# A gated-delta recurrence and a mixture of experts on one core: chunks of 64 tokens in 12 turns in place of 32 tokens in 24

## The chip, the core and the metric

The kernel runs on one core of a Trainium2 chip. The metric is the time of the whole kernel in microseconds on the device. Engines in the profile: PE is TensorE's matmuls and PEld its weight loads, DVE is VectorE, ACT is ScalarE, POOL is GpSimd, SP issues most of the transfers.

## What is computed

A DeltaNet layer (4 batches, 8 heads, 768 tokens, head size 48) is followed by a mixture of 8 experts with one expert per token. All is float32.

```python
for t in range(S):
    y[:, :, t] = einsum('bhd,bhde->bhe', q[:, :, t], state)
    v_old = einsum('bhde,bhd->bhe', state, k_n[:, :, t])
    state = state + beta_t * einsum('bhd,bhe->bhde', k_n[:, :, t], v[:, :, t] - v_old)
x = y.transpose(0, 2, 1, 3).reshape(3072, 384)
expert = argmax(x @ w_gate);  gate = softmax(x @ w_gate)[expert]
out = gate * (relu(x @ w1[expert]) @ w2[expert])
```

`k_n` is k divided by its length. The 32 pairs of batch and head are independent; the tokens of a pair depend on each other through `state` (48 x 48).

## The kernel before, in words

**Chunks and turns.** The 768 tokens of each pair are cut into chunks of C = 32 tokens, and all 32 pairs take one chunk in one of NT = 24 turns. In a chunk, the sequence of single steps becomes matrix work: the keys' products with each other (scores, L255) give a lower triangular matrix; its inverse (`invert`, L309 to L375) is applied to what the values lack against the state. Partitions are four groups of 32 rows, the columns are 8 pairs (FQ) of 48.

**One turn**, in the order in which the parts need each other: the state times keys and, for the outputs of the chunk before, the state times queries (`with_state`, L456, 128 matmul records into banks BR and BY); VectorE subtracts this from the scaled values, R (L489); the inverse times R and, interleaved with it, the masked products that complete the outputs of the chunk before (L502 and `masked`, L463); ScalarE copies the result as Z (L513); keys times Z are added to the state (`kz`, L518) in two banks that hold the state throughout; ScalarE copies it out as S (L526). Beside it `output` copies the finished outputs, stores them to `xs` in DRAM, transposes them (L549), multiplies them by the gate weights (L562), and `route` finds each token's expert and place (L594 to L645).

**Inverse.** `invert` works on four chunks at a time (a block, six in all): VectorE transposes the scores (L309), finds the lengths of the keys, and eliminates 31 columns with two operations each (L355 and L360). For the first block it eliminates two halves of 16, which TensorE then joins (`couple`, L397 and L404). Scores run up to 12 turns ahead (AHEAD, with RING = 14 buffers).

**Experts.** When all tokens are routed, the lists are loaded, tokens are gathered by list, transposed (L740), and each of 8 experts runs two dense products (L754, L800) for up to 416 tokens; a loop behind it serves more. The weights of the first two experts are loaded during the turns, the third's after.

**Order.** Each operation is entered in a `Plan` with an engine, an estimated duration and a priority; `order` plays a schedule through and writes the instructions in the order of the planned starts. An engine executes in that order. `mode` adds 0.12 us in the plan when TensorE changes its tiling.

## Time and profile before

| | us |
|---|---|
| median of 3 runs | 690.65 (689.38 to 692.21) |
| the profiled execution | 689.81 |
| its span, first to last instruction | 688.1 |
| first Z / last Z | 51.93 / 346.32 |
| first product of an expert | 383.88 |

The profile describes one execution, which took 689.81 us, of which the span covers 688.1. A float32 product leaves two matmul records and a transpose one. In rows of the windows by stage the columns are the stretch and its length, then for each engine busy time and number of instructions, the mean granted clock of TensorE (1.00 is full), the share of time in which the DMA engines were busy, and the GB/s that they moved. In rows of the timeline they are the start, the duration, engine, line, operation, operands and count, and in brackets the idle time ahead and what ended it; "issue" stands where the trace shows nothing that was waited for. Queue rows have packets, megabytes and share of time.

### The profile page before, as it was taken

The page shows a single profiled execution, that of the slowest core. Times are in us where ns is not written, and L with a number is a line of the kernel's source. Part 1 is how long each engine was busy: PE and PEld are TensorE (multiplying, and loading weights), DVE is VectorE, ACT ScalarE, POOL GpSimd, SP SyncE. Part 2 cuts the span into 40 slices and gives each one's busy share as a digit, 9 for nine tenths or more (in the row PEclk, how much of TensorE's full clock was granted, in tenths as well). Part 3 has the DMA queues.
Part 4 walks back from the last instruction along what each step waited for, and adds up shares of the span by engine and source line. Part 5 has one row for each costly group of instructions (what it writes and reads, how often), then busy time and mean ns, then how long its engine had stood idle before and what let it go on. Part 6 is the DMA issues. An engine that isn't in the chain of part 4 may idle for free. (4 is left out here: it accounts for less than half of the span.)

```text
span 688.1 us, 24689 instructions
## 1 busy us (share of the span) xinstructions
PE 539.0 (78%) x11376; PEld 371.4 (54%) x11377; DVE 234.1 (34%) x728; ACT 116.7 (17%) x267; POOL 133.2 (19%) x157
## 2 busy tenths in 40 slices
PE   3575665678587767678770899999999999999992
PEld 2464555567476656567660555555555555555551
DVE  3886755886877662001010101021011101021110
ACT  1222232213222122122210101101110101010100
POOL 1123111122232120210202504030302222101111
PEclk9999567557765655555555899999999999999997
DMA  8406544453322134331010324243433322000000
GB/s 311 157 5 212 162 126 140 144 169 82 106 50 55 51 61 116 96 95 40 15 26 13 92 104 150 92 144 103 143 114 112 102 101 97 23 15 23 13 12 23
DMA packets 36075, 63.58 MB, mean 92 GB/s; under 512 B 6102, under 2 KB 27014, under 8 KB 35968
## 3 DMA queue, kind: packets, MB, share of 16 engines
q1 hardware_dynamic: 30928, 51.62, 24.6%
q0 software_dynamic: 4352, 9.47, 4.2%
q8 instruction: 90, 1.47, 0.9%
q10 hardware_dynamic: 688, 0.88, 0.4%
q14 instruction: 17, 0.14, 0.1%
HBM read 52.68 MB, written 10.05 MB: 91 GB/s over the span
## 5 line engine op out<-in xcount | busy, mean ns | idle before, releaser
L754 PE MATMUL bk<-kqA,w 128*128 128x416 f32 x288 | 102.7, 515 | 0.0
L800 PE MATMUL bk<-w,kqA 128*128 128x384 f32 x288 | 96.1, 490 | 0.0
L754 PEld LDWEIGHTS bk<-kqA,w 128*128 128x128 f32 x288 | 54.5, 192 | 45.0 <-issue 43.3
L355 DVE SCALAR_TENSOR_TENSOR bk<-blkA,b 128x60 f32<-128x60 f32 (+22 forms) x185 | 76.8, 415 | 4.6
L800 PEld LDWEIGHTS bk<-w,kqA 128*128 128x128 f32 x288 | 53.7, 190 | 42.5 <-issue 7.5
L255 PE MATMUL bk<-kqA 64*32 64x64 f32 (+1 forms) x1792 | 47.5, 272 | 29.8 <-issue 19.6
L502 PE MATMUL bk<-R,blkA 32*32 32x48 f32 x1472 | 45.3, 252 | 26.4 <-issue 22.7
L759 DVE TENSOR_SCALAR kqA<-bk 128x416 f32<-128x416 f32 x32 | 18.9, 591 | 133.9 <-PE bk L754 110.4
L711 POOL DMA_INDIRECT out<-y,rows x24 | 23.9, 994 | 206.5 <-ACT y L773 162.6
L456 PE MATMUL bk<-S,kqA 64*32 64x48 f32 x2944 | 48.4, 270 | 13.4 <-issue 11.3
L255 PEld LDWEIGHTS bk<-kqA 64*32 64x32 f32 x1792 | 38.7, 150 | 35.6 <-issue 22.8
L463 PE MATMUL bk<-Z,P 32*32 32x48 f32 x1536 | 46.5, 253 | 14.4 <-issue 14.4
L360 DVE TENSOR_TENSOR blkA<-blkA,bk 128x60 f32<-128x60 f32 (+22 forms) x185 | 54.1, 312 | 2.7
L456 PEld LDWEIGHTS bk<-S,kqA 64*32 64x32 f32 x2944 | 41.0, 138 | 22.1 <-issue 14.8
L518 PE MATMUL bk<-Z,kt 32*48 32x48 f32 x1472 | 37.9, 277 | 18.6 <-issue 11.1
L502 PEld LDWEIGHTS bk<-R,blkA 32*32 32x32 f32 x1472 | 36.1, 128 | 28.4 <-issue 23.5
L489 DVE TENSOR_TENSOR R<-vn,bk 128x384 f32<-128x384 f32 x23 | 12.7, 553 | 107.1 <-PE bk L456 100.3
L463 PEld LDWEIGHTS bk<-Z,P 32*32 32x32 f32 x1536 | 37.1, 129 | 19.6 <-issue 19.6
L518 PEld LDWEIGHTS bk<-Z,kt 32*48 32x48 f32 x1472 | 33.0, 185 | 23.2 <-issue 12.6
L436 POOL TENSOR_TENSOR vn<-v,nt 128x384 f32<-128x384 f32 x24 | 21.0, 877 | 121.0 <-DVE R L489 103.0
L645 POOL DMA_INDIRECT lists<-ent,ri x24 | 24.2, 1007 | 98.0 <-DVE ri L633 61.5
L770 DVE TENSOR_SCALAR y<-bk,rows 128x384 f32<-128x384 f32 x8 | 4.9, 618 | 92.1 <-PE bk L800 92.1
(103 smaller groups left out, 576.1 us busy)
## 6 DMA issues: line engine op xcount, KB each, us to landing
kqA<-in_kq SPq DMA_DIRECT2D x20, 512.0 KB, 7.2
w<-in_w SPq DMA_DIRECT2D x18, 512.0 KB, 5.8
w<-in_w SPq DMA_DIRECT2D x12, 768.0 KB, 5.5
kt<-in_ktok SPq DMA_DIRECT2D x24, 192.0 KB, 2.6
v<-in_vtok SPq DMA_DIRECT2D x24, 192.0 KB, 3.4
xs<-x SPq DMA_DIRECT2D x48, 96.0 KB, 2.6
blkA<-in_w SPq DMA_DIRECT2D x6, 512.0 KB, 4.8
blkA<-in_w SPq DMA_DIRECT2D x4, 768.0 KB
```

Of the source, the lines that this page charges most:

```text
L255: nc.tensor.matmul(dst[32 * q : 32 * q + 32, f, :].rearrange("p (k c) -> p k c", c=32), lhsT=v[rows, 0, x * FQ + f, :], rhs=v[rows, ks[0] ...
L355: dve(m * w, lambda col=col, hi=hi, lo=lo, m=m, w=w, pv=pv: nc.vector.scalar_tensor_tensor(out=pv, in0=gl[:, col + 1 : hi, col : col + 1]. ...
L360: dve(m * w, lambda col=col, hi=hi, lo=lo, w=w, pv=pv: nc.vector.tensor_tensor(out=u[:, col + 1 : hi, lo : lo + w], in0=u[:, col + 1 : hi, ...
L436: lambda: nc.gpsimd.tensor_tensor(out=v2s[t % 3][:], in0=vs[t % 3][:], in1=nt[:, u * FQ : u * FQ + FQ].unsqueeze(2).to_broadcast([128, FQ, ...
L456: nc.tensor.matmul(dst[quad(col), f, :], lhsT=KQ(t)[64 * e : 64 * e + 64, k, x * FQ + f, :], rhs=Sbs[t % 2][64 * e : 64 * e + 64, x, f, :] ...
L463: nc.tensor.matmul(sh(BY)[quad(q ^ 2), f, :], lhsT=Pbs[t % RING][quad(q), f, :], rhs=Zbs[t % 2][quad(q), f, :], start=start, stop=True, sk ...
L502: nc.tensor.matmul(pz[quad(q), f, :], lhsT=tt[quad(q), u * FQ + f, :], rhs=Rv[quad(q), f, :], start=True, stop=True,)
L518: nc.tensor.matmul(sh(BS[x])[64 * e : 64 * e + 48, f, :], lhsT=kt[quad(q), f, :], rhs=Z[quad(q), f, :], start=(t == 0 and f == 0), stop=Tr ...
L645: P.op("POOL", 1.0, lambda i=i: nc.gpsimd.indirect_dma_start(out=lists, out_offset=bass.IndirectOffsetOnAxis(ap=ri[:, i : i + 1], axis=0), ...
L711: nc.gpsimd.indirect_dma_start(out=out, out_offset=bass.IndirectOffsetOnAxis(ap=idx, axis=0), in_=src, in_offset=None, bounds_check=N - 1, ...
L754: nc.tensor.matmul(bk[b][:, 0:CAP], lhsT=a1[:, s, f * 128 : f * 128 + 128], rhs=xT[:, s, :], start=(s == 0), stop=(s == NK - 1))
L800: nc.tensor.matmul(bk[b][:, 0:DM], lhsT=hT[:, f, t * 128 : t * 128 + 128], rhs=a2[:, f, :], start=(f == 0), stop=(f == NF - 1))
```

## The change

Chunks have 64 tokens (C = 64), in NT = 12 turns. The partitions of a product are two groups of 64 rows, one for each e, and the outputs go to two groups of 64 and to a pair of adjacent banks, one for each e. PSUM is four pairs: state, residual (BR), inverse (BZ) and outputs (BY). Scores share BY with the outputs; transposes, logits and ranks share BZ with the inverse.

A turn solves its 64 tokens in two steps of 32. The values enter BR by two products with the identity (`values`); the state times keys is added to them in place; VectorE and ScalarE copy one bank each as R; the first half's inverse gives Z; `across` adds the coupling of the halves to BR; R is copied again; the second half's inverse gives the rest of Z; then kz and S as before. The outputs' products with the state and with the masked scores are now separate groups of 64 records. The keys' signs and the order of the halves are turned for odd e, so that the rows of each product lie in their own lanes.

`invert` takes two chunks of 64 as a block, still six blocks, with diagonal 32 x 32 blocks that four DMAs collect in `GD`. The scaling by beta comes ahead of the elimination, the products of the elimination lie in SBUF instead of PSUM, and the first block is eliminated whole; `couple` is gone. RING is 6 and AHEAD is 4. The weights of the first three experts take buffers of the recurrence and are loaded when these are free. Keys and queries are loaded without zero rows, in four transfers a turn. In the plan, `mode` gives way to `passes`: after every 128 matmuls the next block can't end before 3.4 us.

The core of the diff, with the new side of the turn:

```diff
-C = 32
+C = 64
...
-NB = NT // 4
+NB = NT // 2
...
-RING = 14
-AHEAD = 12
+RING = 6
+AHEAD = 4
+PAGE, FILL = 128, 3.4
...
-            eng, cost, _, _, _, mode, lat = self.ops[i]
-            if mode is not None and mode != last.get(e):
-                cost += 0.12
-                last[e] = mode
+            eng, cost, _, _, _, passes, lat = self.ops[i]
             start[i] = t
+            end = t
+            if passes:
+                each = cost / passes
+                while passes:
+                    k = min(passes, PAGE - page)
+                    end += k * each
+                    passes -= k
+                    page += k
+                    if page == PAGE:
+                        page = 0
+                        end = max(end, filled)
+                        filled = end + FILL
+            else:
+                end += cost
+            free[e] = end
...
+    pairs = [pp.tile([128, 2, 512], FP32, name=f"pair{i}") for i in range(4)]
+    bk = [pairs[i // 2][:, i % 2, :] for i in range(8)]
+    BS, BR, BZ, BY = 0, 2, 4, 6
...
+            for g in range(2):
+                P.op("PE", 0.9, lambda g=g: run(BY, (0, 1), range(4 * g, 4 * g + 4)), r=kKQ(t), w=kb(BY),
+                     prio=t - AHEAD + 0.5 + 0.01 * g, passes=32)
+                src = pairs[3][:].rearrange("p e (f c) -> p e f c", f=4)
+                P.op("ACT", 0.6, copy(
+                    "ACT",
+                    xy[:, :, 16 * u : 16 * u + 16].rearrange("p c (e f) -> p e f c", e=2)[:, :, 4 * g : 4 * g + 4, :],
+                    src[:, :, :, 0:C]),
+                    r=kb(BY), w=[("XY", n % 3, u, g)], prio=t - AHEAD + 0.5)
+                P.op("ACT", 0.6, copy("ACT", Pm(t)[:, :, 4 * g : 4 * g + 4, :], src[:, :, :, C:]),
+                     r=kb(BY), w=[("P", t % RING)], prio=t - AHEAD + 0.5)
+        later = const("later").rearrange("p (e c) -> p e c", e=2).unsqueeze(2).to_broadcast([128, 2, FQ, C])
         P.op(
...
+        for q in range(4):
+            s = q % 2
+            e, k = (nc.scalar, "ACT") if n == 0 and s else (nc.sync, "SP")
+            P.op(k, 0.6, dma(e, flat(GD[quad(q)]), flat(xy[quad(q), 32 * s : 32 * s + 32, :])),
+                 r=kXY(n), w=[("GD", q)], prio=pr - 3, lat=2.3)
...
+            r, w = slice(16 * h, 16 * h + 16), 16 * h + 16
+            dve(16 * w, lambda r=r, w=w: nc.vector.tensor_tensor(
+                out=gl[:, r, 0:w], in0=gl[:, r, 0:w], in1=b[:, r].unsqueeze(2).to_broadcast([128, 16, w]),
+                op=OP.mult), [K("b")], [kgl], pr)
+        dve(32, lambda: nc.vector.tensor_copy(out=flat(u)[:, 0:1024:33], in_=b[:]), [K("b")], [ku], pr)
+        for j in range(31):
+            m, w = 31 - j, j + 1
+            pv = prods[n % 2][:, 0 : m * w].rearrange("p (a b) -> p a b", b=w)
+            dve(m * w, lambda j=j, m=m, w=w, pv=pv: nc.vector.tensor_tensor(
+                out=pv, in0=gl[:, j + 1 : 32, j : j + 1].to_broadcast([128, m, w]),
+                in1=u[:, j : j + 1, 0:w].to_broadcast([128, m, w]), op=OP.mult),
+                [kgl, ku], [("prod", n % 2)], pr)
+            dve(m * w, lambda j=j, w=w, pv=pv: nc.vector.tensor_tensor(
+                out=u[:, j + 1 : 32, 0:w], in0=u[:, j + 1 : 32, 0:w], in1=pv, op=OP.subtract),
+                [("prod", n % 2)], [ku], pr)
...
+    def with_state(t, bank, k, first):
+        for f, e, x in products():
+            nc.tensor.matmul(
+                sh(bank + e)[half(x), f, :], lhsT=KQ(t)[feat(e), k, x * FQ + f, :],
+                rhs=Sbs[t % 2][feat(e), x, f, :], start=first and f == 0, stop=True,
+                skip_group_check=True,
+            )
...
+        def values():
             for e in range(2):
+                nc.tensor.matmul(
+                    bk[BR + e][:, 0:DM], lhsT=const("ident"),
+                    rhs=v2s[t % 2][:, e * FQ : e * FQ + FQ, :].rearrange("p f d -> p (f d)"),
+                    start=True, stop=True, skip_group_check=True,
+                )
+        P.op("PE", 1.3, values, r=[("v2", t % 2), "cf"], w=kb(BR), prio=t - 0.3, passes=4)
         if t:
+            P.op("PE", 1.0, lambda: with_state(t, BR, 0, False), r=kKQ(t, (0,)) + kS, w=kb(BR), prio=t, passes=64)
+        def residual(i):
+            for e in range(2):
+                P.op("ACT" if e else "DVE", 0.45, copy(
+                    "ACT" if e else "DVE", Rbs[i][:, e].rearrange("p f d -> p (f d)"), bk[BR + e][:, 0:DM]),
+                    r=[("bk", BR + e)], w=[("R", i, e)], prio=-90)
+        def inverse(i):
+            def run():
+                for f, e, x in products():
+                    q = 2 * x + (e ^ i)
                     nc.tensor.matmul(
+                        sh(BZ + e)[quad(q), f, :], lhsT=tt[quad(q), 16 * u + 8 * e + f, :],
+                        rhs=Rbs[i][quad(q), e, f, :], start=True, stop=True, skip_group_check=True,
                     )
+            P.op("PE", 0.8, run, r=kT + [("R", i, e) for e in range(2)], w=kb(BZ), prio=t, passes=64)
+            P.op("ACT", 0.75, copy("ACT", both(Z), two(BZ), -1.0), r=kb(BZ), w=[("Z", t % 2)], prio=-90)
+        def across():
+            for f, e, x in products():
+                q = 2 * x + e
+                nc.tensor.matmul(
+                    sh(BR + e)[quad(q ^ 1), f, :],
+                    lhsT=xy[quad(q), 32 * (1 - e) : 32 * (1 - e) + 32, 16 * u + 8 * e + f],
+                    rhs=Z[quad(q), e, f, :], start=False, stop=True, skip_group_check=True,
+                )
+        residual(0)
+        inverse(0)
+        P.op("PE", 0.8, across, r=kXY(n, (u,)) + [("Z", t % 2)], w=kb(BR), prio=t, passes=64)
+        residual(1)
+        inverse(1)
         if t < NT - 1:
             def kz():
+                for f, e, x in products():
                     nc.tensor.matmul(
+                        sh(BS + x)[feat(e), f, :], lhsT=kt[half(x), e * FQ + f, :],
+                        rhs=Z[half(x), e, f, :], start=(t == 0 and f == 0), stop=True,
                         skip_group_check=True,
                     )
+            P.op("PE", 1.2, kz, r=[("kt", t % 2), ("Z", t % 2)], w=kb(BS), prio=t, passes=64)
+            for x in range(2):
+                P.op("ACT", 0.45, copy(
+                    "ACT", Sbs[(t + 1) % 2][:, x].rearrange("p f d -> p (f d)"), bk[BS + x][:, 0:DM]),
+                    r=[("bk", BS + x)], w=[("S", (t + 1) % 2, x)], prio=-90)
+    def output(t):
         if t:
+            P.op("PE", 1.0, lambda: with_state(t, BY, 1, True), r=kKQ(t, (1,)) + [("S", t % 2, x) for x in range(2)],
+                 w=kb(BY), prio=t + 0.6, passes=64)
+            P.op("ACT", 0.2, copy("ACT", between[:].rearrange("p (e f) -> p e f", e=2),
+                                  two(BY).rearrange("p e (f d) -> p e f d", d=D)[:, :, :, 0]),
+                 r=kb(BY), w=["between"], prio=-80)
+        def masked():
+            for f, e, x in products():
+                nc.tensor.matmul(
+                    sh(BY + e)[half(x), f, :], lhsT=Pm(t)[half(x), e, f, :], rhs=Zbs[t % 2][half(x), e, f, :],
+                    start=(t == 0 and f == 0), stop=True, skip_group_check=True,
                 )
+        P.op("PE", 1.0, masked, r=[("P", t % RING), ("Z", t % 2)], w=kb(BY), prio=t + 0.6, passes=64)
+        for h in range(2):
+            i = 2 * t + h
+            P.op("ACT", 0.45, copy(
+                "ACT", xbs[i % 3][:].rearrange("p (e c) -> p e c", e=2),
+                pairs[BY // 2][:, :, 192 * h : 192 * h + 192], -1.0),
+                r=kb(BY), w=[("x", i % 3)], prio=t + 0.6)
+            P.op("SP", 0.6, dma(nc.sync, xs[i * 128 : i * 128 + 128, :], xbs[i % 3][:]),
+                 r=[("x", i % 3)], w=[("xs", i)], prio=t - 3)
+    def logits(t):
+        for h in range(2):
+            i = 2 * t + h
+            x, xT, b = xbs[i % 3], xTs[i % 2], BZ + h
+            def tx(x=x, b=b):
+                for s in range(NK):
+                    nc.tensor.transpose(
+                        bk[b][:, s * 128 : s * 128 + 128], x[:, s * 128 : s * 128 + 128], const("ident"))
+            P.op("PE", 0.7, tx, r=[("x", i % 3), "cf"], w=[("bk", b)], prio=t + 1.2, passes=6)
+            P.op("ACT", 0.45, copy("ACT", xT[:].rearrange("p a b -> p (a b)"), bk[b][:, 0:DM]),
+                 r=[("bk", b)], w=[("xT", i % 2)], prio=t + 0.7)
+            def lg(xT=xT, b=b):
+                for s in range(NK):
+                    nc.tensor.matmul(bk[b][:, 0:E], lhsT=xT[:, s, :], rhs=wg[:, s, :], start=(s == 0), stop=(s == NK - 1))
+            P.op("PE", 0.6, lg, r=[("xT", i % 2), "wg"], w=[("bk", b)], prio=t + 1.2, passes=6)
+            m, j = group_of[i]
+            P.op("ACT", 0.2, copy("ACT", lgs[m % 2][:, j, :], bk[b][:, 0:E]),
+                 r=[("bk", b)], w=[("lg", m % 2, j)], prio=t + 0.7)
...
+    weights(0, 8)
+    weights(1, 20)
     weights(2, 21)
```

## The prediction

> **What bounds the kernel now.** I read the time slices of the page first, then the windows by stage, then TensorE's timeline, then the instruction queue. The first view splits the 688.1 us span.
>
> ```profile
> core 0: us, PE busy (x) PEld busy (x) DVE busy (x) ACT busy (x) POOL busy (x), PEclk, DMA share, GB/s
> 0.00:52.00 52.00, 27.64 (x1370) 24.56 (x1372) 35.30 (x123) 10.48 (x25) 10.31 (x23) 1.00 0.44 156
> 52.00:347.00 295.00, 206.76 (x8819) 176.93 (x8813) 156.27 (x503) 70.08 (x172) 56.29 (x66) 0.62 0.36 100
> 347.00:385.00 38.00, 15.44 (x198) 12.35 (x199) 6.13 (x40) 3.17 (x9) 11.26 (x12) 0.50 0.16 38
> 385.00:660.00 275.00, 274.26 (x951) 149.62 (x950) 35.13 (x60) 31.76 (x61) 51.57 (x53) 1.00 0.26 87
> ```
>
> Four stages: a start until the first inverse is there (first Z at 51.9 us), the recurrence, the routing tail (last Z at 346.3, first expert product at 383.9), and the experts (304.2 us to the end, TensorE 100% busy at clock 1.00). The change touches only the first three. In the recurrence TensorE is busy for 207 of 295 us, so it is neither full nor waiting for one engine. Its own timeline says what the rest is.
>
> ```profile
> 42.80 1.03 PE L404 MATMUL bk<-v,blkA 32*16 32x16 f32 x101 [0.93 <-issue]
> 43.77 1.06 PE L255 MATMUL bk<-kqA 64*32 64x64 f32 x26
> 46.36 1.28 PE L255 MATMUL bk<-kqA 64*32 64x64 f32 x38 [1.54 <-issue]
> 47.58 1.54 PE L397 MATMUL bk<-blkA 32*32 32x16 f32 x90
> ...
> 53.27 1.03 PE L404 MATMUL bk<-v,blkA 32*16 32x16 f32 x102 [1.23 <-issue]
> 54.23 0.87 PE L518 MATMUL bk<-Z,kt 32*48 32x48 f32 x26
> ```
>
> Between the stops are 127, 128 (38+90) and 128 (102+26) matmul records, whatever the product; with a stop at 49.82 the stops end 3.45 to 3.57 us apart. "issue" means that nothing in the trace was waited for. The queue table explains it:
>
> ```profile
> q8 instruction: 90, 1.47, 0.9%
> ```
>
> That is 16 KB a packet, 1.47 MB over TensorE's 22,753 instructions (records plus weight loads), so one packet per 126 records: TensorE waits for its own code, one block per 3.45 us at best. Between 60 and 347 us I add up 70.8 us of such stops against 13.5 us of idle time behind R, Z, S and other work. So the recurrence is bound by the matmul count: its busy time, plus stops set by blocks of 128.
>
> **The matmul count.** Each f32 product leaves two records (L754: 384 = 8 experts x 8 x 3 x 2), a transpose one. Before, start to routing: 1792+2944+1536+1536+1472+96+384+96+512 = 10,368 records (L255, L456, L463, L502, L518, L549, L562, L612 with L618, L397 with L404), 81 blocks. After, 12 turns: scores 896, values 48, state-into-residual 704, two inverses 1536, across 768, kz 704, state-into-output 704, masked 768, transposes 72, logits 144, ranks 96: 6440, 50 blocks. A late turn has 478 records (7 x 64 and values, transposes, logits, ranks), 3.7 blocks, 12.9 us at 3.45 us each; a turn with scores 542 and 14.6 us.
>
> Here the Trainium skill speaks against the change. "Runtime: NRT & Kernel Launch", section Instruction fetch mechanics, says that code is streamed ahead in 16 KiB blocks and that crossing a block boundary is mostly hidden, since issue is slower than the fill. Then fewer instructions would remove no stop: 71 us of stops spread over 11 turns (6.5 us each) would stay, and with half of the waits below inside them a turn would be 19.1+6.5+1.0 = 26.6 us, the whole 678. The rows show stops at the boundaries, so I let them shrink.
>
> **Work per turn of 64 tokens.** Late in the recurrence a product of 64 records on four tiles is seen alone:
>
> ```profile
> 349.02 1.50 PE L456 MATMUL bk<-S,kqA 64*32 64x48 f32 x64
> 350.46 1.03 PE L562 MATMUL bk<-wg,xT 96*64 96x8 f32 x16
> ```
>
> kz (64 records, four tiles) takes 1.53 as well; the old state product with 128 records on eight tiles took 1.79. The new tiles are fewer and larger, so half the records do not mean half the time. At clock 0.5:
> - two inverses, across, kz: 4 x 1.4 (1.5 less an overlapped end) = 5.6 us.
> - the three products with 64-wide weights: 1.4 each if the width is free; the L562 row (64-wide weights, two tiles, about 0.1 us each) gives up to 1.95. I take 1.8: 5.4 us.
> - values: 4 full-array records of 384 columns, L800's 96.1/288 = 0.33 us at full clock, 0.67 at half: 2.7 us.
> - transposes 6 x 0.265 (L549, 1.06 for four) = 1.6; logits with 128-wide weights 12 x 0.235 (six L612 records in 1.42) = 2.8; ranks (11.5+11.3)/24 = 0.95 a chunk, 1.9 us.
> Sum 20.0 us. Scores: 32 records of 64 columns on four tiles took 1.06, 26 ns each; twice the columns, 64 records: 3.4 us, in about six of the 11 intervals. Before, two turns held about 2 x (1.8+2.05+1.5+1.1+1.0)+1.9 = 16.8, with scores 21: arithmetic on TensorE hardly falls.
>
> The clock is the second open size. By the Trainium skill, "TensorE: Matmul & The Clock Gate", Part 1, one busy window of about 3.4 us releases the full clock and an idle one takes it back. The trace half agrees: 252.0 to 255.5 us is busy for 3.49 us and the next window has 0.98; 339.5 to 343.0 is busy for 3.50 and the next has 0.50. A burst of the inverse products at a recorded full clock (from 202.05) sends some 85 records in 0.64 us, 7.5 ns each, against 12 at 344.5 to 346.0. Fully by the rule, a denser TensorE would need about 0.62 of these durations (12.4 and 14.5 us); by the last 90 us of this recurrence, busy for three quarters at clock 0.50, all of them. I take two thirds of the work as slow: 17.5 and 20.5, mean 19.1 us.
>
> Waits: five products in a row need evictions between them: R 0.5+0.2 twice, Z of 768 columns about 0.8+0.2 twice (384 take 0.49, 512 take 0.59), S two of 0.49. 4.5 us, covered by values, scores, masked, transposes; without cover all 4.5. I charge 2 us uncovered plus 1.5 us of code stops. Mean turn 22.6 us.
>
> **VectorE** is the floor. The inversion has as many and as large steps per block as now: 62 two-operand steps. L360's forms summed over 31 steps give 10.35 us; twice, plus 0.03 between steps, 22.6; with transposes, square roots, scaling 31 us a block, 15.5 a turn; R copies 1.0, routing 1.6, POOL collisions 1.5: 19.6. As RING is 6, the inverse can't run far ahead, so a turn below 19.6 is excluded. Both operands now lie in SBUF; L355 at 247 columns shows 636 ns against 494 at 255, which I read as collision with POOL, so it may also cost up to 2 us more. The R copies make VectorE wait for the state product with the inversion's steps queued behind them; the third of an interval that is left covers that.
>
> **Start.** Block 0 goes through an SBUF copy by DMA (four issues on SP and ACT, 2.6 us as xs<-x), which the earlier end of two chunks' scores pays for. On SP this copy waits for the scores, and the later kq loads stand behind it; the prologue has two more turns loaded than it needs, so I count nothing (bounds 0 and 3 us). From 13 us: small steps 5.0 (13.56 to 18.59 now), scaling 1.2, chain 22.6, transposes 2.0, inverse 1.6: first Z at 45.5, 6.4 us earlier; couple goes. Bounds 41 to 52. **Tail.** Output with state is done ahead of the last Z, two chunks go through transposes and logits instead of one, and two list scatters instead of one follow the last rank (now 3.2 to 4.3 us apart). I count 34.5 us instead of 37.6. The first three experts' weights, 3 MB each, are moved behind the recurrence: of their fifteen SP issues the first five come free after turn 9, the other ten with 6 MB follow the last turn, at the 360 GB/s of the first slices 17 us, beside the lists on the same engines; the list loads stand behind them on SP. Covered by routing's 20 us; without that cover plus 6. ACT's copies of scores (four of 0.59) and POOL's mask (1.95) and value scale (1.5) per turn fit. SP issues per 64 tokens: 10 now (kq 2, kt 2, v 2, xs 4), 10 after (kq 4, kt 1, v 1, xs 2, block copy 2); no change.
>
> **Sum.** 45.5 + 11 x 22.6 + 34.5 + 304.2 = 632.8 us span; the profiled execution took 689.81 for 688.1, so 634.5. That execution lies 0.8 below the median of 690.65 shown; I predict 634. The break-even turn is (688.1-384.2)/11 = 27.6 us.
>
> **Rivals.**
> - VectorE binds, clock mostly full: 19.6 us a turn, 384.2+215.6+1.7 = 601. For: 156 us of VectorE in 295 now. Against: scores stop its R copies.
> - TensorE stays at half clock but covered: mean 21.9+3.2 = 25.1: 662. For: 0.50 from 260 us on.
> - The change doesn't do what it says, stops remain as large: 678.
> - Slower: one mechanism, shared PSUM. Scores and outputs now share BY, and logits and ranks share BZ with the inverse; before they had own banks (BC, BX). Through BZ a turn pushes transposes, copy, logits, copy, two banks staggered: 4.9 us, and every second turn ranks 3.8 us, in the gap between the second Z and the next inverse. If every eviction stands uncovered behind the in-order TensorE, a turn is 21.9+4.5+1.9 = 28.3: 384.2+311+1.7 = 697. It decides from 27.6 on. For: wherever R is late now, TensorE stands. Against: kz, S, ks and R leave 5.3 us there.
>
> **Chances.** Main 0.43, VectorE floor 0.15, half clock 0.18, stops remain 0.08, shared PSUM 0.16. A difference of 0.5%, 3.5 us, is about what a measurement here can tell from none; within it 0.03 (edge of the last two). Faster 0.81, slower 0.16. Range 598 to 688: from the floor to just short of the shared-PSUM case.
>
> **What would show it.** Instruction packets near 60 instead of 90; issue idle in the recurrence below 30 us; Z pairs 20 to 25 us apart; first Z at 42 to 48; a mean clock above 0.62; experts 304 us. I am wrong if Z pairs lie over 27 us apart, with TensorE waiting for R or Z or with state products over 2 us, or if the first expert product comes over 45 us after the last Z.

## The result and the profile after

| | before | after |
|---|---|---|
| median (four runs each) | 690.01 | 664.99 (662.37 to 670.60) |
| ratio, 95% interval | | 0.9643 (0.9575 to 0.9711) |
| the profiled execution, its span | 689.81, 688.1 | 670.60, 668.8 |
| first Z / last Z | 51.93 / 346.32 | 58.52 / 291.36 |
| first product of an expert | 383.88 | 354.72 |

The change gains 25 us, where the forecast was 56. Medians are taken over all runs and ratios over the fast ones alone, so a ratio need not be the quotient of two medians. The profiled execution is the slowest of the four. I set the terms of the sum, which came to a span of 632.8, against its span of 668.8:

| stage | predicted | measured | difference |
|---|---|---|---|
| start, to the first Z | 45.5 | 58.5 | +13.0 |
| first Z to last Z | 248.6 | 232.8 | -15.8 |
| last Z to first expert product | 34.5 | 63.4 | +28.9 |
| experts to the end | 304.2 | 314.1 | +9.9 |

The second row hides two errors that partly cancel. The forecast counted eleven turns from one first Z to the next; these took 224.4 us, 24.2 less than 248.6. But each turn now has two Zs, and the sum has no term for the stretch from the last turn's first Z (282.91) to its second, which is the last Z: 8.4 us.

First the stages again, as windows of the changed kernel (columns as for the kernel before), and its row of the queue table.

```profile
core 0: us, PE busy (x) PEld busy (x) DVE busy (x) ACT busy (x) POOL busy (x), PEclk, DMA share, GB/s
0.00:59.00 59.00, 23.62 (x516) 18.67 (x517) 42.86 (x99) 15.39 (x21) 17.02 (x17) 0.79 0.66 163
59.00:292.00 233.00, 202.43 (x5792) 170.76 (x5792) 173.49 (x527) 82.67 (x175) 51.14 (x38) 0.68 0.33 96
292.00:355.00 63.00, 23.56 (x145) 20.62 (x146) 5.92 (x44) 4.33 (x14) 15.65 (x16) 0.50 0.34 108
355.00:640.00 285.00, 280.68 (x961) 152.67 (x961) 35.06 (x61) 31.88 (x61) 51.01 (x52) 0.99 0.25 83
...
q8 instruction: 59, 0.97, 0.7%
```

In the recurrence TensorE is busy for 202 of 233 us; before it was busy for 207 of 295. Its work did not shrink: its stops went. There are 59 packets of code instead of 90. Adding up the idle times of TensorE's timeline that end in "issue", I find 7.9 us between 60 and 292 us, where the kernel before had 70.8 between 60 and 346; waits for other engines rose from 13.5 to 21.1. What is left looks like this, in TensorE's timeline of a late turn:

```profile
243.88 0.71 PE L469 MATMUL pair<-R,blkA 32*32 32x48 f32 x25 [2.02 <-issue]
245.52 1.50 PE L479 MATMUL pair<-Z,blkA 32*32 32x48 f32 x64 [0.92 <-ACT Z L230]
248.23 1.50 PE L469 MATMUL pair<-R,blkA 32*32 32x48 f32 x64 [1.21 <-DVE R L232]
```

One stop of the old kind, then the waits that the five products in a row bring: 0.92 us for Z, 1.21 for R.

The tail is read from POOL's timeline, whose rows L623 are the list scatters:

```profile
305.89 0.97 POOL L623 DMA_INDIRECT lists<-ent,ri  x1 [23.03 <-DVE ent L619]
313.42 0.97 POOL L623 DMA_INDIRECT lists<-ent,ri  x1 [6.56 <-DMA lists<-ent,ri]
...
337.46 0.97 POOL L623 DMA_INDIRECT lists<-ent,ri  x1 [3.56 <-DMA lists<-ent,ri]
```

Eight scatters follow the last Z, each waiting for the landing of the one ahead. Four belong to the tiles 16 to 19, whose tokens were done two turns earlier: `route` enters its second part one turn late, and the last turn's inverses, in the same bank, stand ahead of it. Before, four scatters followed the last Z (346.32), the first and the last of them at:

```profile
356.96 0.97 POOL L645 DMA_INDIRECT lists<-ent,ri  x1 [18.39 <-DVE ri L633]
...
367.94 0.97 POOL L645 DMA_INDIRECT lists<-ent,ri  x1 [3.31 <-DMA lists<-ent,ri]
```

So the last scatter goes out 46.1 us behind the last Z instead of 21.6, which is nearly all of what the tail grew.

The start is read from VectorE's and POOL's timelines:

```profile
24.02 1.34 DVE L390 TENSOR_TENSOR prod<-blkA 128x31 f32<-128x31 f32 x1
25.40 0.21 DVE L394 TENSOR_TENSOR blkA<-blkA,prod 128x31 f32<-128x31 f32 x1
...
26.73 1.95 DVE L390 TENSOR_TENSOR prod<-blkA 128x112 f32<-128x112 f32 x1
28.71 0.28 DVE L394 TENSOR_TENSOR blkA<-blkA,prod 128x112 f32<-128x112 f32 x1
```

```profile
23.74 1.58 POOL L414 TENSOR_TENSOR vn<-v,nt 128x768 f32<-128x768 f32 x1 [4.34 <-DMA v<-in_vtok]
26.54 2.01 POOL L323 TENSOR_TENSOR pA<-pA,cf 128x1024 f32<-128x1024 f32 x1 [1.22 <-ACT pA L230]
```

The first elimination step takes 1.34 us instead of 0.2, the seventh 1.95 instead of 0.28, and each ends within 0.15 us of the POOL operation beside it. Five such steps in the first chain and one before it take 8.7 us more than the same steps alone. VectorE's first step on the copied block starts at 16.49 instead of the 13 that I took: 3.5 us.

### The profile page after: what moved, and what is told of

It is laid out like the page before. It is cut to its first block, busy times and chain, and to the rows that moved or that the text cites. A ratio compares the mean times of both kernels' runs of the same rounds, so it can differ in the third digit from the quotient of the medians.

```text
span 668.8 us, 16727 instructions
## 1 busy us (share of the span) xinstructions
PE 542.2 (81%) x7448; PEld 368.9 (55%) x7449; DVE 258.5 (39%) x732; ACT 135.4 (20%) x271; POOL 138.6 (21%) x127
## 5 line engine op out<-in xcount | busy, mean ns | idle before, releaser
L736 PE MATMUL pair<-kqA,blkA 128*128 128x416 f32 x240 | 87.2, 523 | 0.0
L390 DVE TENSOR_TENSOR prod<-blkA 128x87 f32<-128x87 f32 (+15 forms) x186 | 78.4, 423 | 4.4
L782 PE MATMUL pair<-blkA,kqA 128*128 128x384 f32 x240 | 80.1, 490 | 0.0
L394 DVE TENSOR_TENSOR blkA<-blkA,prod 128x87 f32<-128x87 f32 (+15 forms) x186 | 72.5, 391 | 4.3
L736 PEld LDWEIGHTS pair<-kqA,blkA 128*128 128x128 f32 x240 | 46.0, 194 | 38.5 <-issue 37.2
L782 PEld LDWEIGHTS pair<-blkA,kqA 128*128 128x128 f32 x240 | 44.8, 190 | 35.4 <-issue 6.3
L469 PE MATMUL pair<-R,blkA 32*32 32x48 f32 x1536 | 35.7, 267 | 31.6 <-DVE blkA L401 19.8
L289 PE MATMUL pair<-kqA 48*64 48x128 f32 (+1 forms) x896 | 43.7, 359 | 20.5 <-ACT pA L230 12.4
L736 PE MATMUL pair<-kqA,pA 128*128 128x416 f32 x144 | 51.0, 514 | 0.3 <-ACT y L755 0.3
L469 PEld LDWEIGHTS pair<-R,blkA 32*32 32x32 f32 x1536 | 30.6, 154 | 36.7 <-DVE blkA L401 20.4
L722 PE MATMUL pair<-cf,kqA 128*128 128x128 f32 x96 | 15.8, 295 | 40.0 <-DMA kqA<-xs,rows 35.1
L782 PE MATMUL pair<-pA,kqA 128*128 128x384 f32 x144 | 48.0, 490 | 0.0
L623 POOL DMA_INDIRECT lists<-ent,ri x24 | 24.0, 1000 | 110.6 <-DMA lists<-ent,ri 51.9
L744 ACT ACTIVATE kqA<-pair 128x416 f32<-128x416 f32 x32 | 16.5, 517 | 121.3 <-PE pair L736 86.9
```

Of the source, the lines that this page charges most:

```text
L289: nc.tensor.matmul(bk[bank + e][half(x), i * w : i * w + w].rearrange("p (k c) -> p k c", c=C), lhsT=v[feat(e), 0, x * FQ + f, :], rhs=v[f ...
L390: dve(m * w, lambda j=j, m=m, w=w, pv=pv: nc.vector.tensor_tensor(out=pv, in0=gl[:, j + 1 : 32, j : j + 1].to_broadcast([128, m, w]), in1= ...
L394: dve(m * w, lambda j=j, w=w, pv=pv: nc.vector.tensor_tensor(out=u[:, j + 1 : 32, 0:w], in0=u[:, j + 1 : 32, 0:w], in1=pv, op=OP.subtract) ...
L469: nc.tensor.matmul(sh(BZ + e)[quad(q), f, :], lhsT=tt[quad(q), 16 * u + 8 * e + f, :], rhs=Rbs[i][quad(q), e, f, :], start=True, stop=True ...
L623: P.op("POOL", 1.0, lambda i=i: nc.gpsimd.indirect_dma_start(out=lists, out_offset=bass.IndirectOffsetOnAxis(ap=ri[:, i : i + 1], axis=0), ...
L722: nc.tensor.transpose(bk[b][:, t * 128 : t * 128 + 128], xv[:, t * DM + s * 128 : t * DM + s * 128 + 128], const("ident"))
```

## The experiments

Four questions: what the code blocks cost, what makes the tail, what makes the start, and what sets a turn. The kernel before, timed beside each group of kernels, took 687 to 695 us from group to group, so times of different groups are compared by their ratio to the kernel before on the same chip.

**The reference.** `a0_unchanged`, no edit.

> The changed kernel as it is, as the measure for the runs beside it: about 665 us, with first Z at 58.5 us, last Z at 291 and first expert product at 355 of the span if the profiled execution of before was typical. If that execution was a slow one, its extra 5 us should be missing here from one stage, and the trace should say from which.

665.93 us, 0.9675 (0.9639 to 0.9711); first Z 59.0, last Z 289.2, first expert product 350.5. The tail is 61.3 us, so both long stages are properties of the kernel and not of one execution.

### Code blocks

`p1_before_pad` (before) and `p2_after_pad` (after):

```diff
+            for i in range(64):
+                q = quad(i % 4)
+                nc.tensor.matmul(bk[BR][q, 400:401], lhsT=const("ident")[q, 32 * (i % 4) : 32 * (i % 4) + 32],
+                                 rhs=cf[q, 0:1], start=True, stop=True, skip_group_check=True)
```

> The kernel before with 64 products more in each of turns 1 to 23, 32 by 32 weights and one moving column into a column that nothing reads, behind the state product of the turn: 128 matmul records of almost no arithmetic. Theory (each block of 128 records costs TensorE 3.45 us in the recurrence of before, whatever the records do): up to 23 x 3.45 = 79 us slower, at least 55, with stops of the kind seen now. Rival (it is the arithmetic and the dependencies of the recurrence that cost the time, and the stops at every 128th record are chance): 128 records at 7.5 to 12 ns are 1.0 to 1.5 us: 23 to 35 us slower at most.

780.09 us, 1.1303 (1.1248 to 1.1357): 90.7 us slower, 3.9 us for each 128 records. The timeline and the queue table of it:

```profile
207.13 0.32 PE L456 MATMUL bk<-S,kqA 64*32 64x48 f32 x15 [2.00 <-issue]
...
208.20 1.17 PE L492 MATMUL bk<-cf 32*32 32x1 f32 x97 [0.19 <-DVE R L496]
210.58 0.48 PE L492 MATMUL bk<-cf 32*32 32x1 f32 x23 [1.22 <-issue]
...
q8 instruction: 113, 1.85, 1.1%
```

97 of the added records take 1.17 us, so 128 of them are about 1.5; a turn grew by 3.9. Exactly 23 packets are added, one a turn, and the stops grow from 70.8 to 122.3 us (from 60 us to the last Z), 2.2 us a turn. The cost is even above the 79 us that I had put as the most. The mechanism on which the gain was forecast holds.

> The changed kernel with the same 128 records more in each of turns 1 to 11, behind the state product. Theory (its recurrence is no longer bound by the blocks: 4 to 5 blocks in 20 us leave room for one more): the records cost only their own issue, 1 to 2 us a turn where VectorE is late and they fill a gap, none: 0 to 20 us slower. Rival (the blocks still set the time): 11 x 3.45 = 38 us slower.

802.96 us, 1.1630 (1.1563 to 1.1696). The outputs are wrong and the lists change, presumably because the added products disturb the sums in the residual's bank, which I did not test; the time behind the last Z says nothing. The rival has the size right: first Z to last Z grew from 230.1 to 271.5 us, 3.8 us a turn; 1.9 us of that are the records themselves (128 in 1.88 us in its timeline), and stops grew from 6.3 to 21.9 us, 1.4 a turn. So stops alone do not set the time, as the rival had it, but the changed kernel has no room for another block either. I was wrong that it had: its turn is full.

### The tail

`e1_route`:

```diff
                     route(m, 0)
-                    if t == NT:
+                    if t == NT or m == 4:
                         route(m, 1)
```

> The ranks and list scatters of the fifth group of token tiles (16 to 19) are entered one turn earlier, right behind its logits. Theory (the long tail is eight list scatters one behind another, because the ranks come a turn late): these four scatters move into the last turn, four instead of eight are left behind the last Z, the last one goes out about 15 us earlier, the tail from last Z to first expert product falls from 63 to about 47 us, and the time by about 13 us (the last turn gives up to 3 us back, since its inverses now stand behind the ranks). Rival (the tail is long because the weights of the second and third expert fill the transfers while the lists are written): the scatters are still slow, the tail falls by 4 us or less. Rival (the logits and ranks of the last turns on TensorE set the tail): below 6 us.

654.97 us, 0.9524 (0.9492 to 0.9556), 11.0 below the reference. POOL's timeline:

```profile
294.95 0.96 POOL L623 DMA_INDIRECT lists<-ent,ri  x1 [2.72 <-DMA lists<-ent,ri]
305.71 0.96 POOL L623 DMA_INDIRECT lists<-ent,ri  x1 [9.80 <-DVE su L612]
313.39 0.97 POOL L623 DMA_INDIRECT lists<-ent,ri  x1 [6.71 <-DMA lists<-ent,ri]
...
322.01 0.98 POOL L623 DMA_INDIRECT lists<-ent,ri  x1 [3.66 <-DMA lists<-ent,ri]
```

The last scatter goes out at 322.0 instead of 333.6 and the tail falls from 61.3 to 49.3 us. The last turn's first Z comes 2.9 us later, behind the ranks, as expected, but its second only 0.6. The late ranks are the largest single cause of the miss that an experiment shows.

`e4_route_weights`, on top of it:

```diff
-    weights(1, 20)
-    weights(2, 21)
     prepare()
     fetch(0)
     fetch(1)
+    weights(1, 26, [("xin", 0, 3)])
+    weights(2, 27, [("xin", 1, 3)])
```

> On top of the earlier scatters of the fifth group: the weights of the second and third expert wait for the first and second expert's tokens (they came right behind the last turn before). Theory (6 MB of weights in the transfer queues slow the list scatters and, behind them, the list loads and gathers): the wait behind the first scatter after the last turn falls from 7.7 us to about 4, the gathers come about 4 us earlier, and the time falls by 4 us against the kernel with the earlier scatters alone (655.0). Rival (a list scatter takes its 4 us whatever else is moved; the weights lose nothing and cover nothing): same time within 2 us, or slower by up to 5 us if the second expert then waits for its weights.

655.45 us, 0.9501 (0.9440 to 0.9562): no gain to be seen. The wait behind the first scatter does fall, from 6.7 us to 2.9 (3.9 from one to the next instead of 7.7), so the weights had slowed it. But the first of these scatters went out 2.7 us later, for a reason that stays open, so that the last is only 1.2 us earlier. And the extra reads order the plan only: the weights went out right behind the list loads, beside the gathers. The rows of the first transposed tile, from the timelines of `e1_route` and of this kernel:

```profile
329.27 1.04 POOL L686 DMA_INDIRECT kqA<-xs,rows  x1 [6.29 <-issue]
...
332.58 0.45 PE L722 MATMUL pair<-cf,kqA 128*128 128x128 f32 x1 [24.85 <-DMA kqA<-xs,rows]
```

```profile
328.05 1.04 POOL L686 DMA_INDIRECT kqA<-xs,rows  x1 [6.25 <-DMA rows<-lists]
...
334.83 0.45 PE L722 MATMUL pair<-cf,kqA 128*128 128x128 f32 x1 [24.43 <-DMA kqA<-xs,rows]
```

From gather to transpose it was 3.3 us; now it is 6.8. The contention is real, and was moved, not removed.

`e7_two_lists` and `e8_banks`, both on `e1_route`:

```diff
-                out=lists, ...
+                out=twin[i % 2], ...
```

```diff
-            ps = bk[BZ]
+            ps = bk[BS + m % 2 if m > 4 else BZ]
```

> On top of the earlier scatters of the fifth group: the lists are written as two, even and odd tiles of a group each in its own, loaded both and merged on VectorE by four small operations, so that a scatter waits for the last but one before it and not for the last one. Theory (a scatter takes 4 us from issue to landing, and the chain of these is the end of the tail: the last four go out at 305.7, 313.4, 317.4, 322.0): the last four go out within about 8 us instead of 16, the list loads come 7 us earlier, the merge costs 1 us: time about 649. Rival (POOL's own work of 1 us a scatter and the transfers beside them set the pace; two open scatters slow each other): less than 2 us, or slower by the merge.

> On top of the earlier scatters of the fifth group: the ranks of the last two groups go to the state's banks, which nothing uses any more after the last state product, instead of the bank that they share with the inverse, the transposes and the logits. Theory (behind the last Z the shared bank makes the last transposes wait for the ranks of the group before: ranks of the sixth group at 300, last transposes only after that): the last scatter goes out 3 to 5 us earlier, time about 651. Rival (the chain output, transposes, logits, ranks, scatter is serial by its data, and the sixth group's scatters hide it): same within 2 us.

Beside these the kernel before took 694.8 us. `e7_two_lists`: 665.53 us, 0.9582 (0.9527 to 0.9636); the last four scatters go out at 324.4, 325.6, 331.2 and 332.5, in 8.2 us instead of 16.3 as forecast, and the tail falls to 43.4 us, but the last Z comes at 306.0, where `e8_banks` on the same chip has 295.9. TensorE's timeline shows part of it: between 60 us and the last Z it has 21 short stops of 0.28 to 0.38 us that end in "issue", most of them after five or six records of an inverse or a coupling, 7.0 us in all, and `e8_banks` has seven, 1.9 us. What makes them, and the rest of the delay, stays open. `e8_banks`: 657.68 us, 0.9461 (0.9417 to 0.9505), 0.7% below `e1_route` and 0.1% below its repeat `e1_again`, which these runs can't tell from none: the rival's "same".

### The start

`e2_mask_wait` and `e3_nomask`, on the changed kernel:

```diff
-            r=["cf"], w=[("P", t % RING)], prio=t - 1.0,
+            r=["cf"] + ([("TT", 0, 1)] if t < 6 else []), w=[("P", t % RING)], prio=t - 1.0,
```

> The masks of the first six turns on POOL (and the scaling of the second turn's values) wait until the first inverse is done. Theory (the first chain of VectorE is stopped by POOL's two-operand work, about 9 us in the first block): first Z moves from 58.5 to about 50 us and the time falls by 6 to 9 us, unless the masks, now one behind another, hold up the first outputs. Rival (the first chain is slow by itself, and the overlap is chance): first Z within 1.5 us of 58.5. Rival (the start is gained, but turns 1 and 2 are bound by the second block's chain and take it back): first Z at 50, but the time falls by less than 3 us.

665.41 us, 0.9680 (0.9648 to 0.9713): the same. First Z comes at 54.3 instead of 59.0, about half of what the theory said, but the masks now lie beside the second chain, and by the seventh turn nothing is left (first Z at 185.1 against 182.5): the second rival.

> The mask on the query scores is left out, so outputs also contain later tokens of their chunk, and the experts' lists differ a little. It takes 12 x 2.0 us of POOL's two-operand work out of the whole recurrence. Theory (POOL's work stops VectorE's elimination steps for about its own duration): the two rows of the elimination, 151 us together in the changed kernel, fall to 130 or less, first Z to 50, and the period of the turns from 20.4 us to 19.3 or so, since VectorE sets it up to turn 9: time lower by 15 to 20 us. Rival (TensorE sets the turns): VectorE's rows fall by the same, first Z comes 8 us earlier, but the period stays at 20.4 us and the time falls by 8 only.

First Z 55.4, third turn's first Z 94.3 instead of 103.1, last Z 279.0 instead of 289.2; VectorE's two rows fall from 152.0 to 134.7 us. (711.58 us in all: more tokens than 416 fell to one expert, and the extra tile's products end its timeline.) Masks cost VectorE 17.3 us, seven tenths of POOL's 24. But 9 of the 10 us that the last Z gains are there by the third turn: from then on the missing masks bring nothing, as the rival said. In the turns behind it something else is the limit.

`e6_start`, on `e1_route`: masks of turns 0 and 1 by VectorE from PSUM while it waits for the block copy; those of turns 2 to 5 behind the second chain.

```diff
+            P.op("DVE", 1.15, lambda: nc.vector.tensor_tensor(
+                out=Pm(t), in0=pairs[3]..., in1=late(FQ), op=OP.mult), ...)
...
+            r=["cf"] + ([("TT", 1, 1)] if t < 6 else []), ...
```

> On top of the earlier scatters of the fifth group (655.0 us, first Z at 59.5): the masks of the first two turns are done by VectorE straight from PSUM, in the time in which it waits for the block copy; the masks of turns 2 to 5 wait on POOL for the second inverse, and the scaling of turn 1's values for the first. So no two-operand work of POOL but one scaling lies beside the first two chains. Theory (POOL's work costs the first two chains about 9 us together, as the kernel without masks showed at turn 2, and after turn 3 TensorE sets the pace, so that it isn't lost again): first Z at 54 to 55 us, the third turn's first Z at 95 instead of 104, last Z at 281 to 283, time 647. Rival (what POOL does not do in the first chains it does in the third, or holds up the outputs and with them the bank that they share with the scores): last Z within 3 us of 289.8, time 653 or more.

659.37 us, 0.9478 (0.9433 to 0.9524), on the chip where the kernel before took 694.8. First Z 53.8, third turn 94.8, as forecast, but the last Z at 295.0; on that chip the turns of `e8_banks`, whose start is unchanged, ended at 295.9. Of 8.2 us at the third turn 0.9 are left: the rival, not the theory.

`b1_all`, all four edits:

> All four edits together on the changed kernel: earlier scatters of the fifth group, masks out of the first two chains, two lists, ranks of the last groups in the state's banks. If they act in different stages, as the theory says (start 8 us, tail 11 + 7 + 3 us), the time is 665.9 less 29: about 637, first Z at 54 to 55, last Z at 282, first expert product at 319. If one takes the place of another, it is between 640 and 648.

660.10 us, 0.9509 (0.9474 to 0.9545), last Z 301.6: a miss; with two lists in it the turns grow as in `e7_two_lists` (17 of the short stops, 5.6 us).

`e1_again` and `b2_first`, on one chip; `b2_first` has the edits of `e1_route`, `e6_start` and `e8_banks`, and the first inverse reads the scaled values directly:

```diff
-                        rhs=Rbs[i][quad(q), e, f, :], ...
+                        rhs=v2s[0][quad(q), e * FQ + f, :] if t == 0 and i == 0 else Rbs[i][quad(q), e, f, :], ...
```

> The kernel with the earlier scatters of the fifth group once more, as the measure for the runs beside it: 0.952 of the kernel before, so about 655 us where that takes 688, with first Z at 59.5, last Z at 290 and first expert product at 339.

> On the changed kernel together: earlier scatters of the fifth group, masks out of the first two chains, ranks of the last groups in the state's banks, and the first turn's first inverse takes the scaled values as they are, without the copy through PSUM for which VectorE waited 2.9 us inside its first chain. Theory (the start is VectorE's chain and what stands in it): first Z at 50 to 51 us instead of 59.5, the second chain 8 us earlier as well, and since TensorE then sets the pace from the same turn on, the time 6 to 9 us below that of the kernel with the earlier scatters alone. Rival (what the start gains is lost again in turns 1 to 4, as with the masks held back before): first Z at 51, time within 3 us of it.

653.14 us, 0.9475 (0.9448 to 0.9503), and 648.71 us, 0.9397 (0.9366 to 0.9428). First Z 50.7 instead of 58.8: 8.1 us; last Z 285.4 instead of 289.2: 3.8. Half of the start is lost again in the turns, between theory and rival. This is the best version: 41 us below the kernel before, and by the ratios 17 to 19 below the changed kernel.

### What sets a turn

`e5_half_chain`, on the changed kernel (tokens beyond an expert's 416 places are left out too):

```diff
-        for j in range(31):
+        for j in range(0, 31, 2):
```

> Every second of the 31 elimination columns is left out (the inverses are wrong, so the outputs are too), and tokens beyond an expert's 416 places are left out, so that no extra tiles run. It takes about 11 us of VectorE out of each of six blocks. Theory (VectorE sets the start and turns 1 and 2; from turn 3 on TensorE at its mixed clock and VectorE are about equal, and the late turns without any inversion already take 18 to 20 us): first Z at 48 us, the third turn no longer waits (29 us becomes 20), the other periods stay at 18 to 21 us, last Z at about 268 us instead of 289: time about 643. Rival (VectorE sets all turns up to the ninth, as the floor of 19.6 us a turn said): the periods fall to 16 or 17 us, last Z below 250, time below 627. Rival (the half clock sets the turns): as the theory, with a mean clock below 0.7 in all stages.

646.93 us; the outputs are wrong, so only the times of the turns are read. The first Z of the third turn and the last Z:

```profile
82.51 0.81 ACT L230 ACTIVATE Z<-pair 128x768 f32<-128x768 f32 x1 [0.45 <-PE pair L469]
...
268.96 0.81 ACT L230 ACTIVATE Z<-pair 128x768 f32<-128x768 f32 x1 [1.65 <-PE pair L469]
```

First Z 47.4, third turn 82.5, last Z 269.0, against 59.0, 103.1 and 289.2. The theory's numbers were 48 and 268. Of the 20.2 us, 20.6 are there by the third turn; from there the two kernels run in step (186.5 and 186.1 us from the third turn's first Z to the last Z), although VectorE has lost some 11 us a block. So from the third turn on VectorE is not the limit. What is left is TensorE, with its clock and with the waits between its products, and `p2_after_pad`, where 3.3 us more of records and stops made a turn 3.8 us longer, fits that.

How its clock goes through one turn, in windows of `e1_again`:

```profile
239.00:246.00 7.00, 3.87 (x159) 3.22 (x157) 5.70 (x27) 1.48 (x3) 0.00 (x0) 0.50 0.18 61
246.00:251.50 5.50, 5.50 (x129) 3.61 (x122) 4.21 (x12) 0.81 (x1) 0.00 (x0) 0.50 0.01 3
251.50:258.50 7.00, 7.00 (x163) 6.70 (x161) 0.56 (x1) 3.35 (x9) 0.00 (x0) 0.98 0.54 167
258.50:262.00 3.50, 3.50 (x132) 3.39 (x131) 0.82 (x5) 0.18 (x1) 0.96 (x1) 0.52 1.02 378
```

With gaps for R and Z, 0.50; after 5.5 us without one, full; then half again. The last window is wholly busy at half clock. The rule that I cited from the Trainium skill ("TensorE: Matmul & The Clock Gate", Part 1: a busy window releases the clock, an idle one takes it back) fits the first three rows and not the fourth by itself: there the clock falls though TensorE has been busy without a gap since 245.7. Whether the small products ahead of the fall (logits and ranks, 8 to 32 columns) count as work for the clock was not tested. Two experiments touch the rest.

`u1_values`, on `e1_route`: the values leave TensorE from turn 1 on.

```diff
+                if t:
+                    P.op("DVE", 0.45, lambda e=e: nc.vector.tensor_tensor(out=Rbs[i][:, e]..., in0=v2s[t % 2]...,
+                        in1=bk[BR + e][:, 0:DM], op=OP.add), ...)
```

> On top of the earlier scatters of the fifth group: from turn 1 on the values no longer enter by identity products; VectorE adds them to both banks when it makes R, as the kernel before did with one. This undoes one part of the change. Theory (TensorE's work sets the turns, and values are 1.6 to 2.9 us of it): TensorE loses 11 x 2.3 = 25 us of work, but R now takes two additions of 0.6 us one behind the other on VectorE instead of two copies beside each other, twice a turn, 11 x 1.2 = 13 us on the path from state to Z: net 5 to 12 us faster, 643 to 650. Rival (values run in gaps that R and Z leave anyway; only the longer path to R counts, with the inversion's steps behind it): 10 to 15 us slower, 665 to 670.

669.67 us (659.42 to 676.24), 0.9732 (0.9686 to 0.9777), beside 0.9475 for `e1_again`: slower by 16.5 us, a little more than the rival said. Its profiled execution is its fastest, and that of `e1_again` its slowest, so the two traces differ by 3.4 us only; but the mean clock of each of its six runs (0.778 to 0.803) lies below each of `e1_again` (0.825 to 0.842). The groups of `e1_again` and then of `u1_values`, and a window of each:

```profile
L449 PE MATMUL pair<-vn,cf 128*128 128x384 f32 x48 | 31.3, 802 | 0.0
L516 PE MATMUL pair<-Z,pA 64*64 64x48 f32 x768 | 26.4, 226 | 0.0
...
100.00:290.00 190.00, 168.32 (x4822) 142.44 (x4822) 139.85 (x422) 67.49 (x145) 45.95 (x36) 0.72 0.33 95
```

```profile
L524 PE MATMUL pair<-Z,pA 64*64 64x48 f32 x768 | 34.9, 264 | 0.0
L501 PE MATMUL pair<-Z,kt 64*48 64x48 f32 x704 | 16.5, 273 | 11.8 <-ACT Z L230 10.7 <-issue 1.0
L449 PE MATMUL pair<-vn,cf 128*128 128x384 f32 x4 | 2.9, 887 | 0.0
...
100.00:290.00 190.00, 162.71 (x4674) 147.31 (x4666) 146.74 (x443) 58.45 (x126) 45.34 (x36) 0.63 0.34 96
```

28.4 us of identity products are gone, but the clock falls from 0.72 to 0.63, the other products of the recurrence and routing together grow by 26.5 us (masked from 26.4 to 34.9), and kz now waits 10.7 us for the second Z, which the identity products had covered. The masked products show that the growth is the clock's: a turn's 64 records take 2.04 to 2.07 us where the granted clock is 1.00 and 3.63 to 3.65 where it is 0.50. In `e1_again` eleven of the twelve groups run at 1.00, in `u1_values` three. So the identity products' work is paid back by what it does for the clock and by the gap that it fills.

`b3_both`, `b2_first` with the same edit:

> The edits of the third kernel of this call and the values added by VectorE. If both theories hold (start minus 7, values minus 8), about 640 us where the kernel before takes 688; if VectorE then sets the turns, because it gets 1.2 us a turn more, no better than the better one of the two.

653.32 us (647.34 to 663.27), 0.9432 (0.9398 to 0.9466): not better than `b2_first`, as the fallback said.

`f4_filler` and `f2_filler`, on `b2_first`, with four and two products of zeros in each place:

```diff
+        for _ in range(4):
+            nc.tensor.matmul(bk[BS][:, 384:512], lhsT=const("ident"), rhs=zero[:], start=False, stop=True, ...)
```

> The best kernel so far (648.7 us where the kernel before takes 689.8), with four products of the identity with zeros, 128 columns each, into unused columns behind the state product, both inverses and the coupling of each turn, where TensorE would wait for R and Z. They add 0.22 us a product at full clock, 0.9 us a place, 12 x 4 x 0.9 = 42 us of work at full clock and twice that at half. Theory (the waits for R and Z take the clock away, and TensorE sets the turns): mean clock from 100 to 290 us above 0.85 instead of 0.70, turns of 16 to 18 us instead of 20.5, last Z 25 to 40 us earlier, time 610 to 625. Rival (the clock follows something else, such as a budget, and the fillers are only work): clock as before, turns 2 to 4 us longer, time 670 to 700.

> The same with two products a place, 0.44 us at full clock, which leaves a gap of about half a microsecond in each wait. Theory of the clock: if any gap takes the clock away, it stays near 0.70 and the time near 648 plus up to 10; if it is the share of busy time[...], the clock rises part of the way and the time is 625 to 640. Rival (fillers are only work): 655 to 670.

661.99 us, 0.9608 (0.9560 to 0.9656), and 653.29 us, 0.9493 (0.9461 to 0.9524). Windows of `b2_first`, `f2_filler` and `f4_filler`:

```profile
100.00:290.00 190.00, 168.87 (x4742) 143.58 (x4744) 137.24 (x413) 66.71 (x145) 46.29 (x36) 0.71 0.32 94
```

```profile
100.00:290.00 190.00, 174.39 (x4680) 152.09 (x4680) 133.71 (x410) 63.49 (x140) 44.80 (x34) 0.79 0.32 92
```

```profile
100.00:290.00 190.00, 171.74 (x4710) 150.44 (x4710) 137.48 (x420) 63.40 (x139) 42.09 (x32) 0.92 0.34 92
```

Filled waits raise the clock from 0.71 to 0.79 and 0.92: the gaps do take it away. But both kernels are slower than `b2_first` (0.9397), so neither the theory's time nor the rival's clock came. With four products a place the group of the inverses and that of the coupling fall together from 51.0 to 41.6 us and the identity products from 32.0 to 22.8, while the fillers themselves are 62.1 us, not the 42 that I had put: a place of four takes 1.16 us at full clock and 1.3 on average, not 0.9. They took more than they gave back. What full clock without fillers would be worth stays open.

## Right and wrong, by the prediction's own steps

The sum came out 36 us of span too low. The start (13.0), the last turn's second Z (8.4), the tail (28.9) and the experts (9.9) were 60.2 us too low together, and the turns 24.2 too high: without that error on the other side, which was luck, the forecast would have missed by more.

- **The matmul count**: right. 59 packets against "near 60", issue idle 7.9 us against "below 30", and the padded kernel before shows the cause. The rule of the Trainium skill that I weighed against it ("Runtime: NRT & Kernel Launch", Instruction fetch mechanics: boundaries mostly hidden) does not hold in this recurrence, where one added block costs 3.9 us a turn.
- **Work per turn and waits**: right in kind and too dear. Turns of 20.4 us between first Zs, 22.6 forecast. Values, 31.3 us in twelve turns of `e1_again`, are 2.6 each, 2.7 forecast; 1.50 us for an inverse, 1.4 to 1.5 forecast. The clock was 0.68, as said (above 0.62). The uncovered waits, 21.1 us from 60 to 292 us, are 1.9 a turn, 2 forecast; what I charged for code stops, 1.5, was 0.7. TensorE's own work was 17.7 us a turn (202.4 us in 233), 19.1 forecast. The last turn's second half, 8.4 us from Z to Z, I left out of the sum without noticing.
- **VectorE's floor**: "a turn below 19.6 is excluded" fell: the mean, 20.4, stayed above it, but single intervals between first Zs take 14.6 to 29.7 us, and the last, without any inversion beside it, 17.9. The floor was an average over turns that do not share it evenly. VectorE binds in the start and up to the third turn's first Z (an interval of 29.7 us, TensorE waiting for the inverse). POOL's collisions cost 17.3 us for the masks alone, 1.4 a turn; 1.5 were forecast, but spread evenly.
- **Start**: the step that failed is "from 13 us" (16.5: the copies of the scores take 1.02 to 1.04 us each and end at 11.6, and the first use of the block copy issued then starts 4.9 us later, where 2.6 were taken for a transfer) and a chain of 22.6 us: it took 31.0, from 24.02 to 55.07. Without the masks beside it and without the first residual (`b2_first`) it takes 24.6 with one collision left. The size of the clean chain was right (24.6 less 1.3 of that collision); I had named the collision ("up to 2 us more") and taken it as small where it lies on the path.
- **Tail**: the step that failed, and the largest, is the count of scatters, "two list scatters instead of one follow the last rank". That is so, but it is not what sets the tail: eight follow the last Z, one behind another, where four did. I had read `route` as before and not asked in which turn its second half is entered and what stands ahead of it in the shared bank; `e1_route` gave back 12 of the 28.9 us. The weights' contention, "covered, else plus 6", was not covered: 4 us at the first scatter, or 3.5 at the gathers. Of the rest the traces show 5 us: the first of the last turn's scatters goes out 15.9 us behind the last Z in `e1_route`, 10.6 in the kernel before, while I had counted the tail 3 us shorter. What remains of the 28.9 stays open.
- **Experts**: taken as unchanged, 9.9 us off. By the trace, the three transposes at each expert's start now stand together in two banks, and the third waits for an eviction, up to 1.18 us at a time (TensorE's waits from the first product on are 4.3 us in `a0_unchanged`, 0.7 before); the first 48 product records take 19.1 us instead of 17.6; and the last output scatter goes out 5.6 us behind the last product instead of 2.4. These were only read, not tried.

The forecast's rivals: shared PSUM (697) is seen only as 4.8 us of waits for `pA`; the full-clock case did not come. That the half-clock case (662) lies next to the measured 665 is chance: its turns were 25.1 us at a clock of 0.50, the measured ones 20.4 at 0.68. The threshold that I had set for being wrong, first expert product over 45 us behind the last Z, is what happened.

## What to carry to other kernels

When a step's granularity doubles, follow every operation that is released by counting steps (here routing, one turn late) to the end of the loop: a lag that was one short step becomes a long one, and at the end nothing hides it. Where the engine stops at every 128th record, counting records told that the stops would go (70.8 us to 7.9 here), but once they are gone the next limit sets the gain, so sum the stages at both ends of the loop as carefully as the loop. Where an engine's clock depends on unbroken work, an operation that fills a wait may cost nothing, and one taken away may gain nothing.

## What the runs showed of the hardware

- An elimination step of VectorE with two operands in SBUF beside a two-operand operation of POOL ends with it: 1.95 us instead of 0.28. Twelve masks, 24 us on POOL, cost 17.3 us of VectorE. It is not only two operands: in `e8_banks` a one-operand step of four columns (TENSOR_SCALAR) takes 1.39 us and ends at 285.77, with POOL's memset (285.75).
- A block of 128 matmul records of almost no arithmetic (97 in 1.17 us) costs 3.9 us in the recurrence of before.
- The same 64 masked records take 2.07 us at a granted clock of 1.00 and 3.65 at 0.50, and twelve turns of them 26.4 us or 34.9, depending on what runs ahead of them; filling TensorE's waits with products of zeros raised the granted clock from 0.71 to 0.92.
- With two lists, two scatters go out in the time of one: pairs of `e7_two_lists` are 4.1 us apart (295.98 and 300.12) and, in the last group, 6.9 (324.35 and 331.22), where single ones of `e1_route` are 3.2 to 4.2 apart in the group before and 7.7 at the same place of the last.
